# A strided convolution with group norm and gelu, forward and backward: first weights over ScalarE's queue, the second batch's affine pass on ScalarE, two more gradient leaves split, a new order

## Chip, core and metric

The kernel runs on one core of a Trainium2 chip. The metric is the device time of one execution, in microseconds (us). Work is done by TensorE (PE, matmuls; PEld is its weight load), VectorE (DVE), ScalarE (ACT) and GpSimd (POOL); SyncE (SP) issues transfers. ACT and POOL issue transfers too, each in order with its other work. Every engine takes its instructions in the order of the program and waits on semaphores for the results of others.

## What is computed

The reference is a 1-D convolution of 31 taps with stride 2, 256 channels in and out, over 2 sequences of 16,000 positions, then a normalisation over time for each channel, a tanh gelu, and the gradients of all four inputs:

```python
def _fwd_reference(x, w, gn_gamma, gn_beta):
    B, T, D = x.shape
    K = w.shape[0]
    s = 2
    L = (T - K) // s + 1
    h = jnp.einsum('blc,cd->bld', x[:, 0:s * L:s, :], w[0])
    for i in range(1, K):
        h = h + jnp.einsum('blc,cd->bld', x[:, i:i + s * L:s, :], w[i])
    mu = jnp.einsum('bld->bd', h)[:, None, :] / L
    var = jnp.einsum('bld->bd', (h - mu) ** 2)[:, None, :] / L
    h = (h - mu) / jnp.sqrt(var + 1e-5)
    h = h * gn_gamma[None, None, :] + gn_beta[None, None, :]
    return _gelu(h)

def reference(x, w, gn_gamma, gn_beta, grad_out):
    _out, _vjp = jax.vjp(_f, x, w, gn_gamma, gn_beta)
    return (_out, *_vjp(grad_out))
```

B = 2, T = 16000, D = 256, K = 31, L = 7985, all in bf16; sums are kept in f32.

## The kernel before

The convolution, its input gradient and its weight gradient are each written as fast FIR trees: a product of polynomials is split in even and odd parts, and three products of half the length (A, the sum or difference part B_, and C_) replace four. Their operands are sums and differences that VectorE forms; the products are "leaves" on TensorE; results of one leaf are added to another's ("seeds", L583 `ve`, L587 `ve_neg`) before it accumulates, in PSUM (`ps`).

The program has five stages, in this order. In each, c counts four chunks of time, and A, B_, C_ the branches.

- F0, forward of batch 0, to about 217 us. `x_load` (L399) fetches x, transposed by the DMA (`turn`, L344); the first chunk's odd rows are loaded plain (L339) in three groups of 128, 128 and 16 partitions and transposed on TensorE (`x_first`, L419). `load_w` (L443) fetches the weights in 16 loads, all on SP, between the x rows and the x turns. `w_sub` (L464) and `f_sums` (L476) form operands, `f_mm` (L508) the matmuls. `f_evac` writes the result out of PSUM with its sum (L611, L616) and its sum of squares (L624); `keep` (L591) copies a partial result out of PSUM, `f_three_b` (L540) and `f_outer` (L573) move others on ScalarE.
- F1, forward of batch 1, to about 450 us, with the gelu and its derivative for batch 0 beside it: `gelu_unit` (L833 to L862), in 16 units of 1024 columns times two halves: ScalarE loads h (`hd`) through its own queue and runs L836, L838, L842, L844, L860; VectorE runs L840, L846, L850, L862.
- G0, input gradient of batch 0, to about 670 us, with the gelu of batch 1 beside it. For each chunk `e_load` (L928) loads the gelu's derivative times the output gradient (`dyd`) and h (`hd`) on SP, 1 MB each. `e_comp` (L932) makes the norm's gradient: for each half of the channels h times s5 plus s6 (L938), dy times s4 (L941), and their sum (L943); then four copies ("spread", L953 on ScalarE or L955 on VectorE) lay it out for the matmuls, and GpSimd copies the edges (L969). `dn_turn` (L977) transposes it and stores it as `dnd` for the weight gradient. `g_mm` (L1033) are the matmuls, `g_three_b` (L1060) and `g_outer` (L1070) moves on ScalarE, L992 operand sums.
- G1, input gradient of batch 1, to about 895 us; `d2_piece` (L1196) forms differences of `dnd` for the weight gradient beside it and stores them as `d2d`.
- W, weight gradient, to the end: nine combinations n of two branches. For each, x and d2 tiles are loaded, `w_add` (L1252) and `leaf_d` (L1413) form operands, and each leaf is either plain (`w_leaf`, 512-column matmuls) or, where (n, branch) is in NODES (L1243), split once more: `w_pairs` (L1360) and `w_single` (L1372) with 256-column matmuls on operands from `pair_x` (L1349) and `pair_d` (L1357), and a copy on ScalarE (L1370). `w_mm` (L1289) are its matmuls; `w_emit` (L1321) adds the last part and stores the gradient through GpSimd's queue.

Nothing of this is run in the order of the text. Each operation is recorded by `Plan.add` (L151) with its engine, a cost and the memory it reads and writes. `Plan.order` (L180) gives each a due time, from the TensorE work that needs it, less a lead by kind, and from a slack where nothing does; then it lists them: whichever engine is free earliest takes, of its ready operations, the one due first, with TensorE held to a window of `look` operations. A transfer is modelled as one server, one transfer after the other; `pads` hold back what follows a transfer. `emit` (L258) pins the result as the program's order on every engine. PACE (L1479) sets when the gelu units of each batch fall due.

Which engine does the spread is one line, for batch 0 and batch 1:

```python
    COPY = ("ACT", "DVE")
```

and a leaf's choice another:

```python
    NODES = {(0, C_), (6, A), (6, C_), (7, A), (8, C_)}
```

## Time and profile before

| | |
|---|---|
| plain runs | 1239.66 us median of 3 (1238.98 to 1240.63) |
| the profiled execution | 1234.47 us; its span 1232.3 us |
| mean granted clock of TensorE | 0.992 |
| busy, share of the span | PE 97%, DVE 82%, ACT 43%, POOL 17% |
| bytes moved | 263.56 MB, mean 214 GB/s |
| TensorE's first matmul, its last VectorE follower | 4.56 us, 1227.67 us |

The profile is of one execution, which was 5.2 us shorter than the median of the plain runs; differences between profiles are to be read against each other and not against the plain times. The waits name the instruction that came last of those that the waiting one needed. An engine that is busy for most of the span bounds the kernel only in the stretches where the others wait for it, so the stages are read apart. Matmuls overlap one another: a 512-column matmul has 379 ns in the record and a 256-column one 273 ns, but the next one starts sooner than that, and what counts is the distance from start to start. The columns of a row of groups are the line, engine, operation, tile names and shapes with the count; busy us and mean ns of one; idle time just before them and what ended it.

### The profile page before, as it was taken

What the parts mean: (1) busy time and instruction counts of PE and PEld (TensorE: products, weight loads), DVE (VectorE), ACT (ScalarE), POOL (GpSimd) and SP (SyncE); (2) the same over time, 40 slices, a digit from 0 to 9 for tenths busy, and PEclk for the clock granted to TensorE, in tenths of its full rate; (3) what the DMA queues carried; (4) which work ended last, traced back from release to release, by engine and by line L of the source; (5) the groups of instructions that cost most, each with busy time, mean ns of one, the idle gap of its engine ahead of it and who ended that gap; (6) DMA issues with size and microseconds to landing.
All of it is one profiled execution on the core that took longest, in us unless ns stands there. A gap on an engine that the chain in (4) does not pass through costs nothing.

```text
span 1232.3 us, 19408 instructions
## 1 busy us (share of the span) xinstructions
PE 1195.2 (97%) x7846; PEld 768.7 (62%) x7846; DVE 1010.3 (82%) x1297; ACT 535.8 (43%) x769; POOL 203.7 (17%) x321
## 2 busy tenths in 40 slices
PE   6999999899999999999999999999999999999998
PEld 4888899577676964444444444444466554566865
DVE  7988798597979859989887889888776986778883
ACT  1243344565768468888783334444322111012200
POOL 1020231011111203211210323333210000011031
PEclk8999999899999999999999999999999999999999
DMA  9642979866695896686636888886899499986562
GB/s 205 108 111 63 191 198 177 168 139 158 127 201 159 258 317 208 231 248 168 213 120 182 254 273 313 245 308 251 300 305 326 145 318 319 320 293 218 179 170 69
DMA packets 283545, 263.56 MB, mean 214 GB/s; under 512 B 186815, under 2 KB 254446, under 8 KB 275184
## 3 DMA queue, kind: packets, MB, share of 16 engines
q1 hardware_dynamic: 255808, 166.38, 52.5%
q0 software_dynamic: 23040, 87.55, 20.1%
q10 hardware_dynamic: 4608, 8.39, 2.3%
q8 instruction: 61, 1.00, 0.3%
q14 instruction: 28, 0.23, 0.1%
HBM read 129.44 MB, written 87.52 MB: 176 GB/s over the span
## 4 chain that ended last, share of the span: by engine, by line
PE 79%; DVE 6%; DMA 6%; issue 4%; ACT 2%; POOL 2%; SPq 0%; POOLq 0%; ACTq 0%; DVEq 0%
PE ps L508 31%; PE ps L1289 27%; PE ps L1033 21%; DMA d2d<-arena 2%; DMA arena<-hd 1%; DVE arena L1196 1%; POOL d2d L341 1%; DVE arena L476 1%; DMA out_dram<-arena 1%; DVE ps L583 1%; DMA arena<-in_x_dram 1%; DVE arena L466 1%; DMA arena<-arena 1%; DMA arena<-in_w_dram 1%; DVE arena L943 0%
## 5 line engine op out<-in xcount | busy, mean ns | idle before, releaser
L1033 PE MATMUL ps<-arena 128*128 128x512 bf16 (+1 forms) x2016 | 435.9, 378 | 11.8 <-DVE ps L583 8.3
L508 PE MATMUL ps<-arena 128*128 128x256 bf16 (+4 forms) x3552 | 426.7, 282 | 12.6 <-DMA arena<-in_x_dram 6.9
L508 PEld LDWEIGHTS <-arena 128*128 128x128 bf16 x3552 | 347.8, 99 | 94.4 <-issue 13.7
L1033 PEld LDWEIGHTS <-arena 128*128 128x128 bf16 x2016 | 198.0, 98 | 249.4 <-issue 20.1
L1289 PE MATMUL ps<-arena 128*128 128x256 bf16 (+1 forms) x2176 | 332.5, 313 | 0.0
L1289 PEld LDWEIGHTS <-arena 128*128 128x128 bf16 x2176 | 212.8, 98 | 112.6
L591 ACT ACTIVATE arena<-ps 128x1024 f32<-128x1024 f32 (+1 forms) x143 | 146.1, 1022 | 277.8 <-PE ps L1033 79.9
L476 DVE TENSOR_TENSOR arena<-arena 128x1087 bf16<-128x1087 bf16 (+3 forms) x194 | 163.7, 889 | 27.5 <-PE ps L508 27.2
L850 DVE TENSOR_TENSOR arena<-arena 128x1024 bf16<-128x1024 bf16 x160 | 109.0, 689 | 14.8 <-ACT arena L842 8.2
L1252 DVE TENSOR_TENSOR arena<-arena 128x4096 bf16<-128x4096 bf16 x42 | 95.8, 2288 | 25.2 <-PE ps L1289 19.6
L583 DVE TENSOR_TENSOR ps<-ps,arena 128x1024 f32<-128x1024 f32 x77 | 94.0, 1229 | 27.0 <-PE ps L1289 13.3
L341 POOL DMA_DIRECT2D out_dram<-arena x75 | 54.1, 741 | 365.7 <-DVE arena L1321 292.0
L992 DVE TENSOR_TENSOR arena<-arena 128x516 bf16<-128x516 bf16 (+3 forms) x176 | 83.5, 513 | 16.4 <-PE ps L1033 10.0
L1196 DVE TENSOR_TENSOR arena<-arena 128x768 bf16<-128x768 bf16 (+3 forms) x112 | 65.5, 642 | 16.7 <-DMA d2d<-arena 15.6
L341 POOL DMA_DIRECT2D d2d<-arena x70 | 51.0, 729 | 112.3 <-DVE arena L1196 110.7
L611 ACT ACTIVATE arena<-ps 128x512 bf16<-128x512 f32 (+1 forms) x64 | 36.8, 578 | 74.5 <-PE ps L508 74.5
L840 DVE SCALAR_TENSOR_TENSOR arena<-arena 128x1024 bf16<-128x1024 bf16 x32 | 39.2, 1224 | 20.1 <-ACT arena L838 19.8
L583 DVE TENSOR_TENSOR ps<-arena,ps 128x1024 f32<-128x1024 f32 x43 | 52.8, 1227 | 3.2 <-PE ps L1033 2.7
L1370 ACT COPY ps<-ps 128x512 f32<-128x512 f32 x28 | 16.0, 571 | 87.6 <-PE ps L1289 87.6
L1060 ACT ACTIVATE ps<-ps 128x512 f32<-128x512 f32 x48 | 27.9, 582 | 58.8 <-PE ps L1033 58.6
L1413 DVE TENSOR_TENSOR arena<-arena 128x2304 bf16<-128x2304 bf16 x36 | 48.0, 1354 | 5.5 <-PE ps L1289 5.5
L341 POOL DMA_DIRECT2D dyd<-arena x32 | 17.6, 550 | 194.2 <-DVE arena L850 189.5
(87 smaller groups left out, 785.8 us busy)
## 6 DMA issues: line engine op xcount, KB each, us to landing
arena<-in_x_dram SPq DMA_DIRECT2D x52, 1024.0 KB, 9.6
arena<-d2d SPq DMA_DIRECT2D x16, 1216.0 KB, 11.9
out_dram<-arena POOLq DMA_DIRECT2D x14, 1024.0 KB, 5.9
d2d<-arena POOLq DMA_DIRECT2D x30, 384.0 KB, 6.3
arena<-dnd SPq DMA_DIRECT2D x10, 960.0 KB, 6.4
vl<-arena POOLq DMA_DIRECT2D x36, 256.0 KB, 4.8
arena<-vl SPq DMA_DIRECT2D x9, 1024.0 KB, 8.6
hd<-arena POOLq DMA_DIRECT2D x8, 1024.0 KB, 6.3
```

The costliest lines, as they stand in the source:

```text
L341: add(eng, issue or {"POOL": 0.8, "SP": 0.4, "ACT": 0.15}[eng], [out], [in_], lambda: e.dma_start(out=out, in_=in_), dma=dcost(nbytes, run ...
L476: lambda: nc.vector.tensor_tensor(out=o, in0=a, in1=b, op=ALU.add))
L508: yield nc.tensor.matmul(ps[:, dh, cs], lhsT=wt, rhs=mv, start=s0, stop=False, skip_group_check=True)
L583: add("DVE", dve(1024, 1), [out], [a, b], lambda: nc.vector.tensor_tensor(out=out, in0=a, in1=b, op=op))
L591: lambda: nc.scalar.activation(out=out, in_=ps, func=ACT.Copy, scale=scale))
L850: add("DVE", dve(1024), [o], [a, b_], lambda: V.tensor_tensor(out=o, in0=a, in1=b_, op=op))
L992: lambda: nc.vector.tensor_tensor(out=o, in0=a, in1=b, op=ALU.add))
L1033: yield nc.tensor.matmul(ps[:, e, 0:wide], lhsT=lt, rhs=mv, start=s0, stop=False, skip_group_check=True)
L1196: lambda: nc.vector.tensor_tensor(out=out, in0=a, in1=b_, op=ALU.subtract))
L1252: add("DVE", dve(4096), [o], [a, b], lambda: nc.vector.tensor_tensor(out=o, in0=a, in1=b, op=ALU.add))
L1289: yield nc.tensor.matmul(ps[:, s, c0:c1], lhsT=lt, rhs=mv, start=s0, stop=False, skip_group_check=True)
L1413: add("DVE", dve(2304), [DL[i3, b]], [D2[b]], lambda b=b, i3=i3, o_=o_: nc.vector.tensor_tensor(out=DL[i3, b], in0=D2[b][:, o_:o_ + 17:2, ...
```

## The change

There are four parts.

1. At the start, the four weight loads of branch A, first half of the channels, and the third group of x rows (16 partitions) are issued from ScalarE's queue and no longer from SP's. SP issues the two other x groups, twelve weight loads and the turns.
2. In `e_comp` for the second batch the affine pass (L938 and L941) becomes activations (Identity, with scale and bias read from memory) on ScalarE, and its spread is done by ScalarE too. The first batch's stays as it was: affine on VectorE, spread on ScalarE.
3. NODES gets (2, A) and (4, A): two more leaves of the weight gradient are split.
4. The planner's listing is rewritten. Transfers of the queues of SP, ScalarE and GpSimd run at once, each queue's one after the other, and share the rate by a weight `tp`; a queue of SP that has more than `room` packets in flight blocks SP's next issue; each kind of transfer has new costs. Slack, look, pads, nearly all leads and PACE have new numbers. So the order of all engines is new.

The counts of the two programs: TensorE 7846 matmuls before and 7918 after (in W 832 of 512 columns become 704, and 1400 of 256 become 1600), VectorE 16 instructions fewer, ScalarE 41 more, GpSimd 321 in both, SP 208 before and 203 after.

The diff, without most of the table of leads and of the listing:

```diff
--- before.py
+++ after.py
@@ -46,82 +46,95 @@
         self.lastw = {}
         self.readers = {}
         self.pe = 0.0
-        self.slack = 120.0
+        self.slack = 100.0
         self.hold = -1
-        self.look = 11
-        self.pads = (270.0, 253.5, 0.0)
+        self.look = 12
+        self.pads = (345.0, 308.5, 1.0)
         self.lead = {
...
-            "F0 load f_evac": 10.5,
-            "F0 load load_w": -2.5,
...
+            "F0 load put": 10.0,
+            "F0 load x_load": -6.5,
...
-            "G1 e_comp conv_stem_kernel": -10.0,
...
+            "G1 e_comp conv_stem_kernel": -12.0,
...
         }
+        self.room, self.mixed = 2048.0, 1.4
@@ -192,68 +205,132 @@
             due[i] = end - full - self.lead.get(o["kind"], 0.0)
+        self.listing(due, succ)
+        return sorted(range(n), key=lambda i: (self.start[i], i))
+
+    def listing(self, due, succ):
...
+        def flow(t):
+            nonlocal now
+            if total > 0:
+                for x in air:
+                    if x["act"]:
+                        x["rem"] -= (t - now) * x["tp"] / total
+            now = t
+
+        def inflight():
+            return sum(x["rem"] * 16e3 / ops[x["i"]]["ns"] for x in air if ops[x["i"]]["eng"] == "SP")
+
+        while done < n or air:
...
+            if best is not None and (event is None or event[0] > best[0]):
+                t, e, w = best
+                flow(t)
+                pick = min((i for i in w if ready[i] <= t + 1e-9), key=lambda i: (due[i], i))
...
+                air.append(dict(i=i, on=False, act=False, lane=turn[k], rem=o["dma"], tp=o["tp"], t0=end + 1.3))
+                lanes[k][turn[k]] = 1
+                turn[k] = (turn[k] + 1) % 8
+                if e == "SP" and inflight() > self.room:
+                    blocked, spend = True, end
+                continue
...
-            if o["dma"] is not None:
-                server = max(server, end + 1.3) + o["dma"]
-                end = server + 0.9
-                lane.append(end)
...
@@ -332,18 +409,20 @@
         names = "abcdefg"[:len(shape)]
         return v.rearrange("p (" + " ".join(names) + ") -> p " + " ".join(names), **dict(zip(names, shape)))
 
-    def dcost(nbytes, run):
-        ns = {256: 18, 512: 27, 1024: 46, 2048: 85, 4096: 165}[run]
-        return nbytes / run * ns / 16e3 * 1.1
-
-    def load(out, in_, nbytes, run, eng="SP", slack=None, issue=None):
+    SH = {256: 36.0, 512: 56.0, 1024: 70.0, 2048: 100.0, 4096: 168.0, 8192: 310.0}
+    PK = {256: 18.0, 512: 28.0, 1024: 46.0, 2048: 84.0, 4096: 168.0, 8192: 310.0}
+
+    def load(out, in_, nbytes, run, eng="SP", slack=None):
         e = {"SP": nc.sync, "POOL": nc.gpsimd, "ACT": nc.scalar}[eng]
-        add(eng, issue or {"POOL": 0.8, "SP": 0.4, "ACT": 0.15}[eng], [out], [in_], lambda: e.dma_start(out=out, in_=in_),
-            dma=dcost(nbytes, run), slack=slack)
+        pk = 8192 if run >= 4096 else 4096 if eng == "POOL" else run
+        np_ = nbytes / pk
+        add(eng, {"POOL": 0.74, "SP": 0.25 + 0.0005 * np_, "ACT": 0.4}[eng], [out], [in_],
+            lambda: e.dma_start(out=out, in_=in_), dma=np_ * PK[pk] / 16e3 * 1.03, ns=PK[pk], tp=SH[pk], slack=slack)
 
     def turn(out, in_, nbytes, slack=None):
-        add("SP", 1.25 + max(0, nbytes - 262144) * 6e-6, [out], [in_],
-            lambda: nc.sync.dma_start_transpose(out=out, in_=in_), dma=dcost(nbytes, 256), slack=slack)
+        np_ = nbytes / 256
+        add("SP", 0.15 + 0.00105 * np_, [out], [in_],
+            lambda: nc.sync.dma_start_transpose(out=out, in_=in_), dma=np_ * PK[256] / 16e3 * 1.03, ns=PK[256], tp=SH[256], slack=slack)
 
     def zero(out, n, eng="POOL"):
         e = {"POOL": nc.gpsimd, "DVE": nc.vector}[eng]
@@ -403,8 +482,9 @@
         src = x[b, 16 * m0:16 * (m0 + nr), :].rearrange("(m e) c -> m (e c)", e=16)
         if b == 0 and c == 0:
             rows = [sb(REG + 4096 * g, 4, 512) for g in range(3)]
-            for g, nm in enumerate((P, P, 16)):
-                load(rows[g][0:nm], src[P * g:P * g + nm].rearrange("m (j o f) -> m j o f", j=4, o=2)[:, :, 1, :], nm * 4096, 1024)
+            for g, nm in ((2, 16), (0, P), (1, P)):
+                load(rows[g][0:nm], src[P * g:P * g + nm].rearrange("m (j o f) -> m j o f", j=4, o=2)[:, :, 1, :], nm * 4096, 1024,
+                     "ACT" if g == 2 else "SP")
             load_w(A)
             load_w(C_)
             x_first(flat, rows)
@@ -451,7 +531,7 @@
                     nq = 4 if i0 + par + 24 < K else 3
                     load(W[br][:, sl, ch, 0:nq, par, :],
                          w[i0 + par:i0 + par + 8 * (nq - 1) + 1:8, ch * P:(ch + 1) * P, :].rearrange("q p d -> p q d"),
-                         65536 * nq, 512, issue=0.8)
+                         65536 * nq, 512, "ACT" if sl == A and ch == 0 else "SP")
 
     def load_gb():
         for i, g in enumerate((gn_gamma, gn_beta)):
@@ -923,7 +1003,7 @@
             load(out.rearrange("(dh p) -> dh p", p=P), DGT[2 * i:2 * i + 2, :], 512, 256, "POOL", slack=500.0)
 
 
-    COPY = ("ACT", "DVE")
+    COPY = ("ACT", "ACT")
 
     def e_load(b, c):
         for t, d in ((EG, dy_d[b][c]), (EH, h_d[b][c])):
@@ -934,11 +1014,17 @@
         for dh in range(2):
             hv, ev = (t[:, dh].rearrange("p e k f -> p (e k f)") for t in (EH, EG))
             s4, s5, s6 = st(b, 4, dh), st(b, 5, dh), st(b, 6, dh)
-            add("DVE", dve(2048, 4), [hv], [hv, s5, s6],
-                lambda hv=hv, s5=s5, s6=s6: nc.vector.tensor_scalar(out=hv, in0=hv, scalar1=s5, scalar2=s6,
-                                                                    op0=ALU.mult, op1=ALU.add))
-            add("DVE", dve(2048, 4), [ev], [ev, s4],
-                lambda ev=ev, s4=s4: nc.vector.tensor_scalar(out=ev, in0=ev, scalar1=s4, scalar2=None, op0=ALU.mult))
+            if b == 0:
+                add("DVE", dve(2048, 4), [hv], [hv, s5, s6],
+                    lambda hv=hv, s5=s5, s6=s6: nc.vector.tensor_scalar(out=hv, in0=hv, scalar1=s5, scalar2=s6,
+                                                                        op0=ALU.mult, op1=ALU.add))
+                add("DVE", dve(2048, 4), [ev], [ev, s4],
+                    lambda ev=ev, s4=s4: nc.vector.tensor_scalar(out=ev, in0=ev, scalar1=s4, scalar2=None, op0=ALU.mult))
+            else:
+                add("ACT", act(2048, 0.18), [hv], [hv, s5, s6],
+                    lambda hv=hv, s5=s5, s6=s6: nc.scalar.activation(out=hv, in_=hv, func=ACT.Identity, bias=s6, scale=s5))
+                add("ACT", act(2048, 0.18), [ev], [ev, s4],
+                    lambda ev=ev, s4=s4: nc.scalar.activation(out=ev, in_=ev, func=ACT.Identity, scale=s4))
             add("DVE", dve(2048), [ev], [ev, hv],
                 lambda ev=ev, hv=hv: nc.vector.tensor_tensor(out=ev, in0=ev, in1=hv, op=ALU.add))
         if c == 3:
@@ -1240,7 +1326,7 @@
     for k, o in (("early", 110720), ("late", 57344)):
         PD[k] = [(sb(o + 4096 * i, 4, 512), sb(o + 8192 + 4096 * i, 2, 4, D)) for i in range(2)]
     LATE = {0: ((0, 94336), (1, 102528)), 8: ((2, 24576), (3, 40960))}
-    NODES = {(0, C_), (6, A), (6, C_), (7, A), (8, C_)}
+    NODES = {(0, C_), (2, A), (4, A), (6, A), (6, C_), (7, A), (8, C_)}
     P1 = [sb(94336 + 4096 * i, 1024, dt=FP32) for i in range(8)]
     P2 = [sb(o, 1024, dt=FP32) for o in (77824, 81920, 182016, 186112)]
     WO = [sb(202816 + 2048 * i, 2, 2, D) for i in range(3)]
@@ -1476,7 +1562,7 @@
 
     RINGS = ((3, 2, 2, 2), (2, 1, 1, 0))
     D2AT = {(0, 0): (0, 1, 2), (0, 1): (3, 4), (1, 0): (5, 6)}
-    PACE = ((5.0, 19.0), (391.0, 67.0))
+    PACE = ((274.0, 3.5), (182.0, 11.5))
     fw = forward()
     load_gb()
     add("DVE", 0.1, [JK], [], lambda: nc.vector.memset(JK, 0.0))
```

More of the change, by code (lines that the diff above doesn't have):

```diff
@@ new lines, in __init__ @@
+            "G0 load e_load": -2.0,
+            "G0 load g_evac": 9.0,
+            "G0 load gelu_unit": 3.5,
+            "G0 load load_w2": 0.5,
+            "G0 spread e_comp": -2.0,
+            "G0 tiny elem_finalize": -11.5,
+            "G0 tiny fwd_stats": 2.5,
+            "G0 tt first": -6.5,
+            "G0 tt gelu_unit": 1.0,
+            "G0 tt second": 7.0,
+            "G0 tt third": 8.0,
+            "G0 turn gelu_batch": -6.5,
+            "G0 ve_neg g_seed": 4.5,
+            "G0 zero e_comp": 0.5,
@@ new lines, in listing @@
+            if blocked:
+                over = inflight() - self.room
+                rate = sum(16e3 * x["tp"] / (total * ops[x["i"]]["ns"]) for x in air if x["act"] and ops[x["i"]]["eng"] == "SP")
+                if over <= 0.0 or rate > 0.0:
+                    t = now if over <= 0.0 else now + over / rate + 1e-9
+                    if event is None or t < event[0]:
+                        event = (t, None)
+            pick = None
+            if best is not None and (event is None or event[0] > best[0]):
+                t, e, w = best
+                flow(t)
+                pick = min((i for i in w if ready[i] <= t + 1e-9), key=lambda i: (due[i], i))
+                if ops[pick]["dma"] is not None and lanes[e == "POOL"][turn[e == "POOL"]]:
+                    pick = None
@@ L232, in order @@
+            free[e] -= self.overlap.get(e, 0.0)
             if e == "PE":
```

221 lines of the change are left out of this document (123 added, 98 removed).

## The prediction

> **What bounds the kernel now.** I read the page's first part, then the stages as windows, then TensorE's waits, then the chain of waits at the two costliest stops.
>
> ```profile
> span 1232.3 us, 19408 instructions
> PE 1195.2 (97%) x7846; PEld 768.7 (62%) x7846; DVE 1010.3 (82%) x1297; ACT 535.8 (43%) x769; POOL 203.7 (17%) x321
> ...
> PEclk8999999899999999999999999999999999999999
> ```
>
> TensorE is the bound: 97% busy, and in slices of 30.8 us its clock is below full only in the first. The stages (columns: window, its length, busy time and count of TensorE, weight loads, VectorE, ScalarE, GpSimd, clock, DMA share, GB/s):
>
> ```profile
> 0.00:31.00 31.00, 20.02 (x136) 13.28 (x137) 22.52 (x28) 3.21 (x3) 3.28 (x11) 0.89 0.91 204
> 217.00:250.00 33.00, 26.89 (x187) 18.95 (x186) 19.51 (x37) 16.37 (x18) 2.92 (x5) 0.90 0.85 164
> 672.00:895.00 223.00, 214.72 (x989) 96.91 (x988) 191.29 (x289) 88.42 (x122) 67.55 (x103) 0.99 0.85 276
> 895.00:1232.00 337.00, 332.63 (x2234) 218.22 (x2231) 252.97 (x203) 55.40 (x67) 30.55 (x41) 1.00 0.75 242
> ```
>
> The weight gradient (last row) never waits: only fewer or shorter matmuls shorten it. Elsewhere there are stops, of which the waits of TensorE name the last releaser (us in total, times, longest):
>
> ```profile
> PE ps L1033 <- DVE ps L583: 8.3, 9, 2.4
> PE ps L508 <- DMA arena<-in_x_dram: 6.9, 2, 4.6
> PE ps L508 <- ACT arena L591: 6.1, 1, 6.1
> PE ps L508 <- DVE arena L476: 4.0, 1, 4.0
> PE ps L508 <- ACT arena L611: 3.5, 2, 1.9
> PE ps L1033 <- ACT arena L611: 2.1, 1, 2.1
> ```
>
> Idle time is not the whole price: after a stop the matmuls run at half clock for a while. From start to start in the trace a 512-column matmul takes 215.7 ns and a 256-column one 109.2 ns (832 x 0.2157 + 1400 x 0.1092 = 332.3 us, the 332.6 of the last stage), and double that in four stretches: 13.9-20.7, 239.1-246.0, 450.8-454.2, 891.1-894.5 us. All starts held against the steady intervals give 1181.4 us of matmul and 41.4 us lost: 9.7 at the start, 8.5 at 235, 2.1 at 317, 1.8 at 388, 4.0 at 448, 1.8 at 464 and 479, 7.3 between 716 and 831, 4.3 at 887, and 1.9 in scraps. Two of these on the chain (start, us, what):
>
> ```profile
> 220.12 15.52 DMA arena<-hd
> 236.86 1.23 ACT arena L838
> 238.11 1.28 ACT L842
> 239.40 1.06 ACT arena L842
> 241.42 72.22 PE ps L508 x528
> ...
> 876.54 9.87 DMA arena<-in_x_dram
> 886.44 2.29 DVE arena L1252
> 888.73 1.15 DVE ps L583
> 889.92 5.30 PE ps L1033 x16
> ```
>
> Queues are first in, first out: at 235 the evacuation L591 that TensorE needs stood in ScalarE's queue behind gelu steps waiting for a load of hd; at 887 an L583 stood on VectorE behind L1252, which waited for raw x.
>
> **Part by part**, against the profiled execution (1234.47 us; its span and 2.2 around it), with the two orders compared.
>
> *Two leaves split.* In the weight gradient 128 matmuls of 512 columns go and 200 of 256 come: 200 x 0.1092 - 128 x 0.2157 = -5.8 us, on an engine without a gap, so all of it counts if VectorE keeps up. VectorE gets 2 L1349 (1.22), 8 L1357 (0.69) and 8 L583 (1.23), 17.8 us, in a stage where it is busy 253 of 337 us; ScalarE 4 copies L1370 (0.57). Uncovered, a late seed stops TensorE. Adding the durations in the new order behind their releasers leaves every VectorE result of combos 2 and 4 on time, the least margin 0.2 us. Value -5.8, bounds -5.8 and +4 (8 seeds late by 1.2 each).
>
> *Order at 235.* The L591 now stands ahead of the gelu steps. Behind them is next the L540 copy, needed 8.9 us of matmul later: hd landed at 232.7 and 235.7, which leaves 9.8 us of gelu steps and evacuations (two L836/L838 pairs, table load, L842, L591, L844, L842, L836, L540), some 1.5 to 2 us late. Stop 2 instead of 8.5: -6.5; bounds -8.5 (hd 2 us earlier) and -4 (2 later, half clock again).
>
> *Order at 317 and 388.* Both L611 stood behind 5 to 6 us of gelu steps with a slack of 2 to 3.5 us. The new TensorE order leaves 6 to 10: -3, bounds -3.8 and 0.
>
> *448 to 480.* The items ahead of L611 are released 2.7 us earlier; an L1060 behind an L624 keeps some 0.8: -3.5, bounds -4.8 and -1.
>
> *Affine pass and spread of the second batch.* Per chunk VectorE loses 2 L938, 2 L941, 2 + 2 L955: 2 x 0.81 + 2 x 0.75 + 2 x 0.56 + 2 x 0.30 = 4.8 us, 19 for four. ScalarE gains 4 activations of 2048 columns. No row shows that: L953's 512 and 1536 columns (0.61, 1.46) extended give 1.89, twice L836 (1.23) gives 2.46; I take 2.2, as these too read scale and bias. With 2 x 1.46 + 2 x 0.61 of copies it is 13.0 us per chunk, 52 for four (47.6 to 56). ScalarE has room in the sum (88 of 223 us) but not in order: L591, L1060 and L1070 run in it, most with 1.72 us between their matmul's end and the need. Two places look late. In chunk 0 an L1060 that must wait for TensorE stands inside the pass, so its sum and turn come 11 us later; and chunk 1's affine pass waits for an hd load, now behind a 960 KB load on SP, and holds evacuations for 2 to 4.6 us, with one half-clock stretch 1.7 more. With 1.2 at the first, 3.3 at the second, 1.2 for chunks 2 and 3, and 0.6 left of the rest, the G1 stops fall from 7.3 to 6.3 (2.3 to 11.3): -1, bounds -5 and +4. Late next is the chunk's turn L977, its store and the dnd load that the L1196 steps read; TensorE stopped 3.3 us behind those at 800 to 831, and I leave it that this can fall or grow within the bounds. GpSimd's L969 copies follow ScalarE's L953 now instead of L955; GpSimd is busy 68 of 223 us there and keeps its 321 instructions.
>
> *Entry to W.* The raw x load goes out ahead of the d2d loads, so 4.3 should vanish; but the d2d loads go 2.4 us later, and VectorE gets 41.7 us of work released within 31 us of matmuls there (26.3 before). Some 2.2 us late: -2, bounds -4.3 and +1.
>
> *Start.* SP issues five loads fewer (15.6 us for 16 w in the timeline), so its four turns of x come some 5 us earlier; ScalarE issues five at 0.33 ahead of its table load, 1.7 us, hidden as its first cast is at 9.86. The first leaf waits at 15.1 for sums of x and w. The window's DMA share is 0.91: what w gains, x loses. x's second group lands about 1 us later and w's first half 1 to 2 earlier: 0, bounds -1.5 and +1.5.
> The Trainium skill ("Trainium Kernel Development and Optimization", Key Constraints) says that transfers issued by SP, ScalarE and GpSimd share the same 16 engines and only issue time is saved. By it the start gains nothing, or at most issue time; by SP's issue row alone it would gain the 4 us of four w issues, and the sum would be 4 lower.
>
> Sum: -5.8 - 6.5 - 3 - 3.5 - 1 - 2 + 0 = -21.8, to 1212.7 by the profiled execution. The three plain runs (median 1239.66) lie 5.2 above it; I forecast such runs, 1239.66 - 21.8 = **1218**, its own range 1208 to 1229.
>
> **Rivals.**
> *Half clock behind the stops that are left.* Stops of 2.12 and 2.40 us (448, 887) brought a stretch of half clock of 3.4 us, that is 1.7 lost; 1.92 and 2.24 (317, 716) did not. I count one for what is left; three more, at 235, in G1 and at the entry to W, give +5: **1223**.
> The Trainium skill ("TensorE: Matmul & The Clock Gate", Part 1) speaks for this one: the window that decides is free-running, so the same stop may or may not bring it. The trace agrees, as the four stops show.
> *The small gains are replaced.* A new order makes its own stops: only the split (-5.8) and 235 (-6.5) hold, G1 takes +4: -8, **1231**. For it: 1.72 us of slack at nearly every G1 evacuation. Against: the slacks at 317 and 388 are read from the order itself.
> *VectorE late in W.* Eight late seeds at 1.2 give +10: -12, 1228. For it: single 31 us stretches with 32 to 34 us of VectorE work. Against: margins at or above 0.2.
> *Slower: ScalarE's queue blocked in G1.* If in all four chunks the affine pass waits for its loads as long as these take to land (6.4 hd, 8.5 dy, median by the list of DMA issues) with evacuations behind it, each stops TensorE some 8.5 us less 1.7 of slack, plus 1.7 of half clock: 4 x 8.5 = 34, less the 20.8 from elsewhere: +13, **1253**. It decides from 5.2 us a chunk on. For it: DMA 0.85 busy at 276 GB/s there, ScalarE strictly in order, where before VectorE took this wait (L938, 3.5 us once). Against: in chunks 2 and 3 the loads are issued early by the new SP order.
> *The change does not act.* The start is one part of which that may hold; it is 0 in the sum already.
>
> **How the numbers follow.** Forecast 0.42, half clock 0.10, small gains replaced 0.20, VectorE late 0.06, ScalarE blocked 0.22. A measurement here can tell 0.2%, 2.5 us. Faster: all of the first two, 0.17 of the third, 0.04 of the fourth: 0.73; same 0.05, the rest of these; slower 0.22. Range: from 1206, a little under the forecast's own, to 1244, which takes in the next three and part of the last.
>
> **What would show it.** Right: 704 matmuls of 512 columns and no gap in W; no idle over 3 us on L591 near 235; L611 gone from TensorE's waits; releasers in G1 turning from DVE L583 to ACT L591 and L1060; the new activation at 1.9 to 2.5 us. Wrong: ScalarE idle on DMA arena<-hd in several G1 chunks with TensorE stopped, gaps in W released by L583, or a first leaf later than 16.6 us.

## The result: slower by 1.6%

The changed kernel takes 1256.82 us (median of 4 runs, 1253.30 to 1259.13) beside 1239.32 us (4 runs, 1237.62 to 1240.63): a ratio of 1.0157 (95% interval 1.0122 to 1.0192). This ratio and those below are estimates from the single runs and not quotients of two medians (here 1.0141). The forecast was 1218, the range 1206 to 1244. The profiled execution took 1258.13 us, 1.3 over its median, where the one of the kernel before lay 5.2 under its own; so the two profiles lie further apart (24 us) than the two medians (17.5). The first lines of its page and its stages (columns as before the change):

```profile
span 1256.3 us, 19516 instructions
...
PE 1192.7 (95%) x7856; PEld 778.1 (62%) x7918; DVE 1005.6 (80%) x1281; ACT 584.7 (47%) x805; POOL 201.9 (16%) x321
```
```profile
0.00:31.00 31.00, 18.95 (x133) 12.96 (x134) 20.50 (x26) 3.21 (x3) 3.29 (x11) 1.00 0.88 204
...
217.00:450.00 233.00, 208.51 (x1594) 158.03 (x1592) 177.22 (x265) 138.68 (x203) 30.56 (x48) 0.95 0.83 173
672.00:895.00 223.00, 215.04 (x973) 97.64 (x992) 174.68 (x272) 131.39 (x150) 66.22 (x104) 0.98 0.81 254
895.00:1256.00 361.00, 348.66 (x2373) 234.83 (x2394) 288.63 (x244) 65.41 (x81) 35.40 (x48) 0.99 0.79 251
```

The trace holds no clock before 21 us, so the 1.00 of the first row is not to be set against the 0.89 of the kernel before.

The program has 7918 matmuls and the record 7856; the 62 missing ones all have 512 columns, which makes a busy TensorE look a little idle. So I measure the stages from first matmul to first matmul, which needs no record in between. Forward (F below): 442.9 us before, 466.2 after. Input gradients (G): 447.6 and 449.5. Weight gradient (W): 332.3 and 330.3. The first matmul starts at 5.34 us in place of 4.56. That is +0.8 + 23.3 + 1.9 - 2.0 = 24.0, the whole difference of the spans. Nearly all of it lies in the forward stages, and 18.2 us of that in three stops of F1. TensorE's waits name the place (the lines have moved: L620 was L540, L663 L583, L671 L591, L691 L611, L916 L836, L1119 L1033, L1375 L1289):

```profile
PE ps L588 <- ACT ps L620: 24.4, 3, 11.5
PE ps L1119 <- DVE ps L663: 9.7, 6, 3.6
PE ps L588 <- DMA arena<-in_x_dram: 9.2, 2, 5.3
PE ps L588 <- DVE arena L556: 2.8, 1, 2.8
PE ps L588 <- ACT arena L691: 2.3, 4, 0.9
```

Three stops on one ScalarE line cost 24.4 us of idle time. The line was in none of the waits before; it is the copy that the prediction named as next behind the gelu steps at 235. With the half clock behind them they cost 14.4 us at 249, 9.0 at 321 and 7.1 at 388; the three stops of the kernel before at 235, 317 and 388 cost 12.3. The first of them in the timeline (start, length, engine, line; in brackets the idle time ahead and what ended it):

```profile
219.94 18.08 SPq L425 DMA_TRANSPOSE arena<-in_x_dram  x1
...
228.34 0.36 ACTq L420 DMA_DIRECT2D arena<-hd  x1
...
249.67 1.24 ACT L916 ACTIVATE arena<-arena,stats 128x1024 bf16<-128x1024 bf16 x1 [18.38 <-DMA arena<-hd]
...
256.58 1.01 ACT L671 ACTIVATE arena<-ps 128x1024 f32<-128x1024 f32 x1
...
260.52 0.58 ACT L620 ACTIVATE ps<-ps 128x512 f32<-128x512 f32 x1
...
261.15 9.11 PE L588 MATMUL ps<-arena 128*128 128x256 bf16 x49 [11.50 <-ACT ps L620]
```

Read it upwards. TensorE waits for L620, which is 0.58 us of work. L620 is late because ScalarE takes its work in order and stood 18.4 us at L916 (the old L836), a gelu step, waiting for a 256 KB load of hd. That load was issued at 228.34 and the step began at 249.67: 21.3 us. Beside it SP was issuing the transposed load of the next chunk of x, from 219.94 to 238. In the kernel before it was 13.2 us from the issue of the load to the step:

```profile
216.92 20.43 SPq L346 DMA_TRANSPOSE arena<-in_x_dram  x1
...
219.53 0.91 ACTq L341 DMA_DIRECT2D arena<-hd  x2
...
232.73 1.24 ACT L836 ACTIVATE arena<-arena,stats 128x1024 bf16<-128x1024 bf16 x1 [10.14 <-DMA arena<-hd]
```

The two other stops of the changed kernel look like its first: an hd load beside an x turn, a gelu step that waits for it (14.8 and 9.6 us), and L671 and L620 behind.

### The profile page after: what moved, and what is told of

Same layout as the page of the kernel before. It is cut to its first block, busy times and chain, and to the rows that moved or that the text cites. A ratio compares the mean times of both kernels' runs of the same rounds, so it can differ in the third digit from the quotient of the medians.

```text
span 1256.3 us, 19516 instructions
## 1 busy us (share of the span) xinstructions
PE 1192.7 (95%) x7856; PEld 778.1 (62%) x7918; DVE 1005.6 (80%) x1281; ACT 584.7 (47%) x805; POOL 201.9 (16%) x321
## 4 chain that ended last, share of the span: by engine, by line
PE 49%; DVE 6%; DMA 6%; issue 4%; ACT 2%; POOL 2%; POOLq 0%; ACTq 0%; DVEq 0%
PE ps L1375 23%; PE ps L1119 21%; PE ps L588 5%; DMA d2d<-arena 3%; DVE arena L1282 2%; DMA arena<-d2d 2%; DVE ps L663 1%; POOL d2d L420 1%; DVE arena L663 1%; DMA arena<-dnd 1%; DVE arena L1338 1%; DVE arena L930 0%; POOL arena L1055 0%; ACT arena L671 0%; DVE arena L1078 0%
## 5 line engine op out<-in xcount | busy, mean ns | idle before, releaser
L588 PE MATMUL ps<-arena 128*128 128x256 bf16 (+4 forms) x3552 | 430.8, 284 | 37.9 <-ACT ps L620 24.4
L1119 PE MATMUL ps<-arena 128*128 128x512 bf16 (+1 forms) x1975 | 435.3, 380 | 14.4 <-DVE ps L663 9.7
L588 PEld LDWEIGHTS <-arena 128*128 128x128 bf16 x3552 | 349.7, 99 | 116.5 <-issue 32.5
L1119 PEld LDWEIGHTS <-arena 128*128 128x128 bf16 x2016 | 198.6, 99 | 250.9 <-issue 22.2
L1375 PE MATMUL ps<-arena 128*128 128x256 bf16 (+1 forms) x2219 | 326.2, 305 | 4.3 <-DMA arena<-d2d 2.1
L1375 PEld LDWEIGHTS <-arena 128*128 128x128 bf16 x2240 | 219.1, 98 | 103.6 <-issue 3.9
L671 ACT ACTIVATE arena<-ps 128x1024 f32<-128x1024 f32 (+1 forms) x143 | 145.6, 1022 | 281.8 <-PE ps L1119 81.8
L556 DVE TENSOR_TENSOR arena<-arena 128x1088 bf16<-128x1088 bf16 (+3 forms) x194 | 164.1, 887 | 11.4 <-PE ps L588 11.4
L1338 DVE TENSOR_TENSOR arena<-arena 128x4096 bf16<-128x4096 bf16 x42 | 95.5, 2287 | 18.6 <-DMA arena<-in_x_dram 17.5
L663 DVE TENSOR_TENSOR ps<-ps,arena 128x1024 f32<-128x1024 f32 x77 | 93.6, 1227 | 20.2 <-ACT ps L1456 8.7
L691 ACT ACTIVATE arena<-ps 128x512 bf16<-128x512 f32 (+1 forms) x64 | 37.0, 580 | 58.4 <-PE ps L588 58.2
L916 ACT ACTIVATE arena<-arena,stats 128x1024 bf16<-128x1024 bf16 x32 | 39.2, 1232 | 43.1 <-DMA arena<-hd 43.0
L663 DVE TENSOR_TENSOR ps<-arena,ps 128x1024 f32<-128x1024 f32 x43 | 52.7, 1226 | 7.8 <-PE ps L588 5.7
L663 DVE TENSOR_TENSOR arena<-arena 128x1024 f32<-128x1024 f32 x32 | 38.7, 1222 | 19.4 <-ACT arena L1156 11.4
L420 POOL DMA_DIRECT2D vl<-arena x36 | 26.1, 727 | 163.5 <-DVE arena L546 85.7
```

The lines of the kernel that those rows point to most:

```text
L420: lambda: e.dma_start(out=out, in_=in_), dma=np_ * PK[pk] / 16e3 * 1.03, ns=PK[pk], tp=SH[pk], slack=slack)
L556: lambda: nc.vector.tensor_tensor(out=o, in0=a, in1=b, op=ALU.add))
L588: yield nc.tensor.matmul(ps[:, dh, cs], lhsT=wt, rhs=mv, start=s0, stop=False, skip_group_check=True)
L663: add("DVE", dve(1024, 1), [out], [a, b], lambda: nc.vector.tensor_tensor(out=out, in0=a, in1=b, op=op))
L671: lambda: nc.scalar.activation(out=out, in_=ps, func=ACT.Copy, scale=scale))
L916: lambda: SC.activation(out=y, in_=h, func=ACT.Identity, bias=bi, scale=sc))
```

## The experiments

Theory A: the loss is made in F1. The new planner reckons that an hd load beside an x turn lands in 3 to 5 us (4.9, 5.2 and 3.3 for the first three loads in its own listing), so it lists gelu steps ahead of evacuations; on the chip the load takes 16 to 21 us, and ScalarE's queue stands. Rivals: the edits of the program cost the time (C), a new listing is tight everywhere (B), VectorE is late in W (D). The kernel before, run beside each group of experiments, had medians of 1235.61 to 1237.19 us. A trace shows one execution, which can lie up to 9 us off the median of its kernel; where it does and the reading hangs on it, the text says so.

### The x turns cut short, in the changed kernel

```diff
-            turn(flat[:, :, 0:nr], src, nr * 8192)
+            turn(flat[:, :, 0:nr], src, nr * 8192, part=(flat[:, 0:2, 0:nr], src[:, 0:256]) if b and c else None)
```
(`part` is what is issued; the planner still sees the whole. Fifteen sixteenths of these chunks of x are not loaded.)

> The changed kernel, every engine's order unchanged, but the three x turns of F1 (batch 1, chunks 1 to 3) move only a sixteenth of their columns, so that later x operands are stale. Theory A1 (hd loads are late because an x turn is in flight beside them): the loads land in 4 to 7 us in place of 16 to 21, L620 no longer stops TensorE, time 1226 to 1236. Rival A2 (they are late because ScalarE issues them 9 us later than before): landings and the three stops stay within 20%, time 1250 or more.

1228.07 us, ratio to the kernel before 0.9923 (0.9896 to 0.9949). The same lines of its timeline:

```profile
217.86 1.19 SPq L425 DMA_TRANSPOSE arena<-in_x_dram  x1
...
226.30 0.36 ACTq L420 DMA_DIRECT2D arena<-hd  x1
...
231.70 1.24 ACT L916 ACTIVATE arena<-arena,stats 128x1024 bf16<-128x1024 bf16 x1 [2.45 <-DMA arena<-hd]
```

The load is issued as late against its neighbours as in the changed kernel and lands in 5.4 us. L620 is gone from TensorE's waits, and F falls from 466.2 to 433.5 us. A1, not A2: a load issued late makes no stop when no long x turn is beside it. The cut takes away the bytes of the turn and its transposing together; no run has a plain load of 2 MB in its place, so which of the two holds the loads is not shown.

### The same cut in the kernel before

The same edit.

> The kernel before, order unchanged, with the same cut as in x_small: the three x turns of F1 move a sixteenth of their columns. Theory A (the loss of the change is how its order stands to the x turns): the stops at 235, 317 and 388, 12.3 us in all, go, 1222 to 1230, and the changed kernel with the same cut (1228.1) lies within 5 us of it. Rival C (the change loses elsewhere too): 1215 to 1220, 8 us or more below the changed kernel with the cut.

1227.20 us, ratio 0.9914 (0.9886 to 0.9942), F 434.3 us. Without the long x turns beside the gelu the two kernels are within 0.9 us of each other, so the net loss hangs on how the two orders stand to the x turns. That is a balance: the changed kernel still has its split (-5.7 us) here, and its W is 2.7 us longer all the same (335.0 against 332.3), with waits for d2d loads at the entry. The stop at 235 goes here too; those at 317 (2.1 us) and 388 (1.8), now at 308 and 380, stay, so they were order alone and no late load.

### The old program under the new planner, the new program under the old one

The one is the changed kernel with the three edits of the program taken back, the other the kernel before with the three made.

```diff
-    COPY = ("ACT", "ACT")
+    COPY = ("ACT", "DVE")
...
-            if b == 0:
+            if b >= 0:
...
-                     "ACT" if g == 2 else "SP")
...
-    NODES = {(0, C_), (2, A), (4, A), (6, A), (6, C_), (7, A), (8, C_)}
+    NODES = {(0, C_), (6, A), (6, C_), (7, A), (8, C_)}
```

> The old program (weights on SP, affine pass and spread on VectorE, five split leaves) listed by the new planner with the new numbers. Theory A (the planner's reckoning of transfers beside each other is what costs): F1 stops as in the changed kernel, 20 us or more on L620 or L611's successors; without the split 5.8 more: 1250 to 1265. Rival C (the three edits of the program cost the time, the order is better): 1225 to 1240.

> The three edits of the program (weights over ScalarE, second batch's affine pass and spread on ScalarE, seven split leaves) listed by the old planner with the old numbers. Theory A: no F1 stop over 9 us; the split's 5.8 are won, what the other two do is within 6 either way: 1228 to 1240. Rival C: 1250 or more, with TensorE waiting for ScalarE in G1.

The old program under the new planner: 1252.84 us, ratio 1.0121 (1.0085 to 1.0157). The line of TensorE's waits and the line of ScalarE's that bear on it:

```profile
PE ps L587 <- ACT ps L619: 17.7, 3, 10.4
```
```profile
ACT arena L915 <- DMA arena<-hd: 41.5, 6, 17.2
```

The three stops are there (13.0, 5.2 and 6.4 us with half clock) without any of the edits: the new planner with its numbers makes them. The other kernel, 1261.06 us (1.0190, 1.0159 to 1.0221), missed what I expected of it. The time is the one of rival C, the place is not: TensorE's waits for ScalarE in the input gradients are 6.4 us. F1's stops are the old ones (6.5, 2.1, 1.8), but there are 14.7 us at the entry to W and 7 more at 947 to 959:

```profile
PE ps L1296 <- DMA arena<-d2d: 11.9, 2, 8.4
...
PE ps L1296 <- DVE arena L1356: 5.6, 2, 3.0
```

The old leads and slacks were numbers for the old program. Listed anew with other durations they lose elsewhere as much. So a program listed anew does not show what an edit is worth by itself; most of the next kernels change the order in place, or not at all.

### Gelu steps behind the evacuations; loads ahead

The first puts ten gelu steps (the expectation says nine) behind the keep and the L620 that they held up, the second puts three hd loads ahead of the statistics step; a sort by start time with some starts overwritten does both, and TensorE's order is the same.

```diff
-        return sorted(range(n), key=lambda i: (self.start[i], i))
+        return self.moved({663: 236.5, 664: 236.6, 679: 236.7, 680: 236.8, 666: 236.9, 698: 236.95, 784: 294.4, 785: 294.5, 891: 348.0, 892: 348.1})
```
```diff
+        return self.moved({662: 216.2, 678: 216.3, 697: 216.4})
```

> The changed kernel with its own order, but nine gelu steps of F1 (the first ones of the three units that waited for hd) are listed behind the keep L671 and the L620 copy that stood behind them; TensorE's own order is untouched. Theory A (ScalarE's queue is blocked by gelu steps whose hd load is late): TensorE's 24.4 us of waiting for L620 fall under 5, with the half clock gone too the time falls by 22 to 28 us, to 1229 to 1235. Rival B (the new order is tight everywhere, the three stops are only where it shows): the gelu chain is late further on, less than 10 us are won, 1247 or more.

1252.75 us, ratio 1.0108 (1.0058 to 1.0158): far from the 1229 to 1235 of theory A. The 24.4 us of waiting for L620 fall to 2.7, as expected, but the evacuation L691 takes 11.0 and two VectorE lines behind the gelu steps 6.3 and 3.2: the stops are now at 260, 277, 334, 342 and 400. The gelu chain keeps three units in flight, each held by its load; what stands behind it on ScalarE changes, that something stands there doesn't. The mechanism of A was right, this cure for it not.

> The changed kernel with one thing moved: the first three hd loads of F1 stand on ScalarE's queue ahead of the statistics step L863 behind which the change had put them; all else as it is. Theory A2 (issued 9 us late): they are issued some 9 us earlier, about 1 us before the x turn's packets, and the stop at 249 (14.4 us) falls to the 8.5 of the kernel before or less: 6 to 10 us shorter, 1244 to 1249 if 1254 is the changed kernel's time. Theory A1 alone (the x turn slows whatever is beside it, wherever issued): landings stay 13 us or more and the stop shrinks by no more than the 9 us of issue, the other two stops (9.0, 7.1) stay.

1247.53 us beside 1236.56 of the kernel before, ratio 1.0065 (1.0022 to 1.0108). The time alone would speak for A2. The timeline does not, but it is of an execution of 1255.62 us, 8 over the median:

```profile
217.56 30.37 SPq L449 DMA_TRANSPOSE arena<-in_x_dram  x1
...
223.49 1.43 ACTq L444 DMA_DIRECT2D arena<-hd  x3
...
245.32 1.24 ACT L940 ACTIVATE arena<-arena,stats 128x1024 bf16<-128x1024 bf16 x1 [16.41 <-DMA arena<-hd]
```

The loads go out only 2.5 us earlier against the x turn's start (5.9 us behind it in place of 8.4), and the first takes 21.8 us; the stop is 12.5. SP's issue of the turn took 30.4 us here, 18.1 in the changed kernel's profile. The two later stops, which nothing touched, were 6.9 and 5.1 in this execution: the landing beside a turn is not a constant, and this kernel's runs reach from 1239 to 1259 us. So why its median is some 9 us under the changed kernel's is not shown; an earlier issue may have its part in it. That a late issue is not needed for so long a stop is shown by p_split below.

### The prediction's step for 235 by itself

In the kernel before, the keep L591 that TensorE waited for is put ahead of the gelu steps; one instruction on one engine moves.

```diff
-        return sorted(range(n), key=lambda i: (start[i], i))
+        return self.moved({970: 225.45, 663: 225.5, 664: 225.6, 679: 225.7, 680: 225.8})
```

> The kernel before with one instruction moved: the keep L591 that TensorE waits for at 235 us stands ahead of the five gelu steps that wait for hd. This is the prediction's step for 235 by itself: the stop falls from 8.5 us to 2, time 1229 to 1233 beside 1236. Rival (the L540 and L591 behind the gelu steps are just as late, the stop moves 5 us of matmul on): within 2 us of 1236.

1237.07 us, ratio 0.9982 (0.9955 to 1.0010): the rival, though the interval still reaches into the step's 1229 to 1233. The trace, of an execution of 1231.58 us, has the stop at 7.6 us in place of 8.5, moved by 18 matmuls:

```profile
242.00 1.22 DVE L607 TENSOR_TENSOR ps<-arena,ps 128x1024 f32<-128x1024 f32 x1
...
243.27 6.92 PE L532 MATMUL ps<-arena 128*128 128x512 bf16 x32 [5.04 <-DVE ps L607]
```

L607 (L583 before) is a seed that stands on VectorE behind gelu steps, which wait for ScalarE's. The prediction had gone by the next evacuation on ScalarE and not by the next result on VectorE.

### The planner mended

The planner let a turn's packets flow only from the end of its issue on SP (9.3 us in its reckoning), and then shared the rate 36 to 100 between a 256-byte packet and a 2048-byte one.

```diff
-    SH = {256: 36.0, 512: 56.0, 1024: 70.0, 2048: 100.0, 4096: 168.0, 8192: 310.0}
+    SH = {256: 400.0, 512: 56.0, 1024: 70.0, 2048: 100.0, 4096: 168.0, 8192: 310.0}
...
-                air.append(dict(i=i, on=False, act=False, lane=turn[k], rem=o["dma"], tp=o["tp"], t0=end + 1.3))
+                air.append(dict(i=i, on=False, act=False, lane=turn[k], rem=o["dma"], tp=o["tp"], t0=t + min(o["dur"], 1.0) + 1.3))
```

> The changed kernel with two numbers of the new planner's reckoning of transfers: a turn's packets flow from the start of its issue and no longer from its end, and a 256-byte turn's weight in the sharing is 400 in place of 36, so that the plan has the first three hd loads of F1 land in 9.5 to 16.5 us (4.9, 5.2 and 3.3 before; the chip 16 to 21). Theory A: F1's three stops fall from 30.5 us to under 15, time 1232 to 1245. Rival B (any new listing makes its own stops): no better than 1250.

> As t0_400 with the weight at 2000: the plan has the loads beside an x turn land in 14 to 25 us, about as the chip does. Theory A: F1's stops under 10 us, 1226 to 1240, faster than t0_400. Rival B: no better than 1250.

With 400: 1240.94 us, ratio 1.0021 (0.9987 to 1.0054). With all three edits and all other numbers as in the changed kernel, F takes 440.2 us in place of 466.2 (in an execution of 1233.83 us, 7 under the median), and of TensorE's waits for ScalarE in the forward stages these are the largest left:

```profile
PE ps L588 <- ACT ps L620: 4.0, 2, 2.8
PE ps L588 <- ACT arena L691: 3.1, 5, 0.9
```

Theory A holds from its other end too: tell the planner what a load beside a turn costs, and the loss in F goes. The gain that was forecast does not come with it: 1.0021, where 1218 us would be 0.98. With 2000, nearest to the chip's landings, F1 has 5.8 us of stops left as expected, yet the time is 1257.52 (1.0116, 1.0047 to 1.0185). Its trace, of an execution of 1248.30 us, loses 28 us in the input gradients (TensorE waits 14.4 for VectorE's seeds), where the kernel before loses 18, and 8 in W, where that one loses nothing. So rival B has its part: each listing also makes stops that nobody planned.

### The edits of the program one by one

Two more split leaves alone, in the kernel before, all orders the same up to the third combination of W:

```diff
-    NODES = {(0, C_), (6, A), (6, C_), (7, A), (8, C_)}
+    NODES = {(0, C_), (2, A), (4, A), (6, A), (6, C_), (7, A), (8, C_)}
```

> The kernel before with the two more split leaves and nothing else, listed by the old planner; all orders are the same up to the weight gradient's third combination. The step of the prediction: -5.8 us, 1229 to 1233 beside 1237.2. Rival D (VectorE late in W): gaps in W released by VectorE, no gain, 1236 or more.

1247.53 us, ratio 1.0093 (1.0061 to 1.0126), rival D. Two places make it. In W a pair difference (L1357) stands at the end of a row of VectorE steps without a gap since 979.8 us:

```profile
996.72 2.49 DVE L1357 TENSOR_TENSOR arena<-arena 128x1024 bf16<-128x1024 bf16 x4
997.55 5.64 PE L1289 MATMUL ps<-arena 128*128 128x256 bf16 x34 [8.16 <-DVE arena L1357]
```

and F1, where no instruction differs from the kernel before, lost 14.9 us at 236 in place of 8.5, because the first hd load took 19.7 us and not 13.2:

```profile
220.85 0.92 ACTq L341 DMA_DIRECT2D arena<-hd  x2
...
240.53 1.24 ACT L836 ACTIVATE arena<-arena,stats 128x1024 bf16<-128x1024 bf16 x1 [16.61 <-DMA arena<-hd]
```

The affine pass and spread alone, issued on ScalarE at the places of the old order (the planner still counts them as VectorE's):

```diff
+                add("DVE", dve(2048, 4), [hv], [hv, s5, s6],
+                    lambda hv=hv, s5=s5, s6=s6: nc.scalar.activation(out=hv, in_=hv, func=ACT.Identity, bias=s6, scale=s5))
...
-                add("DVE", dve(n, 4), [o], [i], lambda: nc.vector.tensor_copy(out=o, in_=i))
+                add("DVE", dve(n, 4), [o], [i], lambda: nc.scalar.copy(out=o, in_=i))
```

> The kernel before, with the second batch's affine pass and spread issued on ScalarE at the very places of the list where VectorE had them. The prediction's step: G1's stops change by -5 to +4 us, 1232 to 1241; the new activation takes 1.9 to 2.5 us. Rival C1 (ScalarE's queue blocked in G1): TensorE waits for ScalarE's L591 or L1060 there by more than 10 us, 1247 or more.

1245.19 us, ratio 1.0077 (1.0038 to 1.0116), between the two. The activation takes 2.0 to 2.1 us. The input gradients take 454.7 us in place of 447.6, that is 7.1 more where the step's upper bound is 4, and TensorE now waits for ScalarE there:

```profile
PE ps L1039 <- ACT arena L591: 6.2, 7, 2.5
PE ps L1039 <- ACT ps L1066: 4.3, 4, 2.5
```

The start alone, loads moved to ScalarE's queue and all else in place:

```diff
-                         65536 * nq, 512, issue=0.8)
+                         65536 * nq, 512, issue=0.8, via="ACT" if sl == A and ch == 0 else None)
```

> The kernel before, with the third x group and the four weight loads of branch A's first half issued from ScalarE's queue, all other orders unchanged. The prediction's step: first leaf within 1.5 us of the 15.1 before, time within 1.5 us of 1237.2. Rival: x's second group lands more than 2 us later and every start with it, 1239 or more.

1237.68 us, ratio 1.0003 (0.9970 to 1.0035): nothing, as forecast. The first leaf starts at 16.6 us (15.1 before), at the very edge of the step's 1.5 us.

In the mended kernel, one edit taken out each (NODES as before; the pass emitted on VectorE where ScalarE had it); and, last, each x turn of F1 issued as four:

```diff
-            turn(flat[:, :, 0:nr], src, nr * 8192)
+            for q in range(4 if b and c else 1):
+                k = 8 if b and c else 32
+                turn(flat[:, k * q:k * q + k, 0:nr], src[:, 128 * k * q:128 * k * (q + 1)], nr * 256 * k)
```

> t0_400 (the changed kernel with the mended reckoning of turns) without the two more split leaves, listed anew. The prediction's term: 5.8 us longer than t0_400, which stood at 1.0021 of the kernel before: 1.004 to 1.009 of it. Rival D (the split costs VectorE what it saves TensorE): 0.999 to 1.003.

1254.54 us, 1.0165 (1.0125 to 1.0204). More than the split's 5.7, but the listing changed in F1 and G too (7.3 us at 308, 4.6 at 665): it prices no term.

> t0_400 with the second batch's affine pass and spread issued on VectorE at the places of the list where ScalarE had them; all other orders the same. The prediction's term (ScalarE's pass is worth 1 us, -4 to +5): 0.999 to 1.006 of the kernel before. Rival C1 (on ScalarE it costs): below 0.998, with TensorE's waits for L671 and L1146 in G gone.

1246.56 us, 1.0101 (1.0063 to 1.0140). TensorE's waits for VectorE's seeds in G are 11.9 us, 5.5 with the pass on ScalarE, and G takes 452.5 us in place of 447.3: in an order made for ScalarE, ScalarE is the better place. Against an order made for VectorE it was not tried, and b_affin, in such an order, went the other way. Not all of the 0.8% between the two is the pass; F1, the same in order, lost 11.0 us at 307 in place of 2.9, again by a longer landing.

> t0_400 with each of the three x turns of F1 issued as four turns of a quarter of the columns, planned one by one. If the length of a turn is what holds the hd loads, ScalarE's waits for hd in F1 fall from 20 us to under 10 and the time to 0.995 to 1.000 of the kernel before. If four short turns in a row load the engines just as one does, landings stay at 10 us and more and the time within 0.5% of t0_400's.

1231.93 us, 0.9976 (0.9950 to 1.0002). The planner puts two quarters at 219 and two at 240 and the loads between:

```profile
219.48 9.00 SPq L425 DMA_TRANSPOSE arena<-in_x_dram  x2
...
225.40 0.36 ACTq L420 DMA_DIRECT2D arena<-hd  x1
...
233.27 1.24 ACT L918 ACTIVATE arena<-arena,stats 128x1024 bf16<-128x1024 bf16 x1 [1.80 <-DMA arena<-hd]
...
240.09 6.09 SPq L425 DMA_TRANSPOSE arena<-in_x_dram  x2
```

The load takes 7.9 us to land, ScalarE waits 4.0 us for hd in all of F1 (18.1 in t0_400), no F1 stop is over 1.2 us, and the ten runs lie within 6.4 us of each other. It is the best version here, 1.8% under the changed kernel by the two ratios; that it beats the kernel before is likely and just not shown, as the interval reaches 1.

## Why the prediction was wrong

The step that failed is the one for 235, and with it the one for 317 and 388: "hd landed at 232.7 and 235.7, which leaves 9.8 us of gelu steps and evacuations". I carried two landing times over from the trace of before into an order in which both the load and the x turn beside it had moved. The load went out 8.8 us later and took 21.3 us, not 13.2. The path was right: ScalarE ran just the listed steps, in 11.4 us from 249.67 to the end of the copy L620; I had put that copy 1.5 to 2 us late, and it held TensorE for 11.5. The 6 to 10 us of slack that I read from the new order at 317 and 388 were likewise counted from releasers among the engines, with the loads taken as there. And in b_behind, with a landing of 12.8 us, the step alone was worth 0.9 us of stop, as a VectorE seed came next.

| step | forecast | between the two profiles |
|---|---|---|
| split, matmul time | -5.8 | -5.7 |
| 235 | -6.5 | +5.9 (8.5 to 14.4) |
| 317 and 388 | -3 | +12.2 (3.8 to 16.1) |
| 448 to 480 | -3.5 | -4.0 (5.8 to some 1.8) |
| G1 | -1 | +2.5 (7.3 to 9.9) |
| entry to W | -2 | +4.1 (4.3 to 8.4) |
| start | 0 | +0.5 |
| new small stops in F0 and F1 | none | +5.3 (L691 2.3 and L663 1.4 by the waits) |
| scraps elsewhere | none | +3.1 |

The forecast missed the difference of the spans by 45.8 us (24.0 against -21.8). The steps at 235, 317 and 388 are 27.6 of it; the entry to W (6.1), new small stops (5.3) and G1 (3.5) come next. So these three are the largest failure and not the only one.

The slower rival had the mechanism and nearly the time (1253): ScalarE's queue, in order, blocked by steps that wait for loads, with evacuations behind them. It had the wrong place, and that its time came near is luck: its 34 us were to arise in G1, which lost 2.5. It was sought where the change adds waits to ScalarE, and there the queue held: the activations took 2.0 to 2.1 us (2.2 taken), pass and spread 48.7 us in all (52 taken; the lower bound of 47.6 should be 46.8 by its own rows), ScalarE's busy time from 672 to 895 us rose from 88 to 131 us, and no more than 2.2 us of TensorE's waits name it. G1's largest stop was VectorE's:

```profile
777.60 1.03 DVE L1282 TENSOR_TENSOR arena<-arena 128x768 bf16<-128x768 bf16 x2 [2.92 <-DMA d2d<-arena]
...
778.54 1.22 DVE L663 TENSOR_TENSOR ps<-arena,ps 128x1024 f32<-128x1024 f32 x1
...
779.67 1.23 DVE L663 TENSOR_TENSOR ps<-ps,arena 128x1024 f32<-128x1024 f32 x1
779.82 10.34 PE L1119 MATMUL ps<-arena 128*128 128x512 bf16 x34 [3.63 <-DVE ps L663]
```

Two seeds behind a difference that waits until a store of d2d has left its buffer. The entry to W (905 us, 6.3 us) has the same pattern, and there the step failed in size: I let the raw x load decide, and the d2d stores and loads did. Why those stores were late in the changed order wasn't tried.

Right were the split's matmul time, the stop at 448, the start (twice, in the changed kernel and in b_queuein) and that VectorE keeps up in W: past the entry, TensorE's waits for it there are 0.6 us in the new order, where a pair difference alone cost 8.2 in the old one (p_split). Of the signs that the prediction named, the idle time on L591 near 235 went, and the time did not follow; the releasers in G1 did not turn to ScalarE. One reading was wrong without effect: the row of the clock is below full in the eighth slice too, where the stop at 235 lies. That I gave the new planner no chance of its own was the gap among the rivals: p_neworder shows that it alone, with its numbers, makes the kernel slower.

## What to carry to other kernels

When a change re-lists a program, the landing times of the old trace are gone with the old order: ask of each load that a step waits for when it is issued now and which large transfer is in flight beside it, before slack is counted. A wait in an in-order queue is cured at its source (the load, or the transfer beside it), since moving what stands behind it only changes the name of what is late (s_behind, b_behind). And a single edit has no price apart from an order: the kernels here that were listed anew moved by stops other than the edit's own, and in place the same pass cost 7 us on ScalarE in the order made for VectorE (b_affin) and 5 us on VectorE in the order made for ScalarE (t_noaff).

## What was not expected of the hardware

A 256 KB load on ScalarE's queue takes very unlike times beside the 2 MB transposed load on SP's:

| kernel | turn issued | load issued | gelu step begins | us | GB/s of all queues meanwhile |
|---|---|---|---|---|---|
| before | 216.9 | 219.5 | 232.7 | 13.2 | 238 |
| p_split, same order there | 218.2 | 220.9 | 240.5 | 19.7 | 184 |
| after | 219.9 | 228.3 | 249.7 | 21.3 | 149 |
| a_loadfirst | 217.6 | 223.5 | 245.3 | 21.8 | 141 |
| t_pieces, half a turn | 219.5 | 225.4 | 233.3 | 7.9 | 190 |
| x_small, a sixteenth | 217.9 | 226.3 | 231.7 | 5.4 | 307 |
| bx_small, a sixteenth | 216.8 | 219.5 | 223.7 | 4.2 | 183 |

The last column is that of the windows from issue to step; two of them (columns as before):

```profile
219.50:232.70 13.20, 13.20 (x99) 9.46 (x98) 3.48 (x12) 1.58 (x2) 1.71 (x3) 1.00 1.13 238
```
```profile
228.30:249.70 21.40, 21.35 (x160) 15.40 (x159) 3.13 (x8) 1.18 (x3) 0.00 (x0) 1.00 1.16 149
```

Time by rate gives 3.1 to 3.6 MB in each of the first four rows, beside 0.8 to 1.7 in the last three. So beside a whole turn the load lands after about the same amount of traffic, and what differs is how fast all queues together move it. A 1 MB store of hd on GpSimd's queue (issued at 226.86 in the changed kernel) is part of that traffic; x_small and bx_small keep it, and the load lands in 4 to 5 us.

A queue of its own does not shield a load. The Trainium skill ("Trainium Kernel Development and Optimization", Key Constraints) says that the queues of SP, ScalarE and GpSimd all run on the same 16 engines and interleave; the trace agrees. The Trainium skill ("DMA: Bandwidth & Descriptors", Queues, rings and completion order) says further that an engine takes turns between its queues packet by packet. Taken alone that would let a small load through soon; 13 to 22 us beside 4 to 5 speak against counting on it. Why the queues together move 238 GB/s in one execution and 184 in another with the same order there stays open. In the four traces with the old order there (before, b_queuein, b_affin, p_split) the load took 13.2, 14.0, 15.1 and 19.7 us, and the stop behind it was 8.5, 8.7, 9.4 and 14.9. That this makes the spread of the kernel before, whose 31 runs beside p_split reach from 1230 to 1249 us, is likely and not shown.
